# Hash-masked attention and a squared-ReLU MLP in one kernel: low planes and hash projections on the two column halves of TensorE

## The chip, the core and the metric

The kernel runs on one core of a Trainium2 chip as one launch. The metric is the device time of that launch in microseconds (us). TensorE (called PE in the profile) multiplies matrices, VectorE is DVE, ScalarE is ACT, GpSimd is POOL, and SyncE (SP) issues most of the DMAs. A matmul on PE has two instructions: a weight load, which the profile counts as an engine row of its own (PEld), and the matmul proper.

## The reference, cut to what matters

```python
q, k, v: (4, 8, 768, 64)      proj: (64, 6)
q_bits = (q @ proj > 0); k_bits = (k @ proj > 0)          # 6 bits a row
mask   = bucket(q_bits)[:, None] == bucket(k_bits)[None]   # same 6 bits
scores = where(mask, 0.125 * q @ k.T, -1e9)
attn   = softmax(scores)       # denominator + 1e-9
x      = (attn @ v)            # heads side by side: (3072, 512)
r      = maximum(x @ w_in, 0)            # w_in (512, 2048)
out    = (s * r * r + b) @ w_out         # w_out (2048, 512), float32
```

There are 32 heads (4 batches of 8), 768 rows a head, head width 64. All inputs and the output are float32, and the signs in the bits make the projections sensitive to small errors.

## The kernel before, in words

**Precision by pieces.** Most matmuls take fp16 or a rounded float32 (`F32R`). Where more precision is wanted, the kernel splits an operand into a high and a low part and multiplies the pieces one after the other: `x @ w` becomes high by high, high by low, low by high. Plain float32 (`F32`) operands go to PE as they are.

**Slots.** A head has three chunks of 256 query rows; a slot is one chunk of one head, so there are 96 slots, with two row tiles of 128 in each. A slot has a part `weights` (lines 554 to 605: scores into PSUM banks, row maximum on DVE at L574, exponential on ACT at L575, normalisation at L595 or L598) and a part `values` (lines 610 to 677: attention weights times v). Heads 0 to 9 (slots 0 to 29) are early, heads 10 to 31 late (`late(w)` is `w >= FULL`, and `FULL` is 10).

**Early values.** The attention weights are transposed on PE (L625), copied out of PSUM (L199) and multiplied in plain float32 (L632). `product(f)` does this for two key tiles at a time: key tile `m` = 0 writes output partitions 0 to 63, `m` = 1 writes 64 to 127, each with 64 weight columns, and two later instructions (L657, L658) add the halves.

**Late values.** ACT scales the normalised weights by `TOP` into an fp16 plane (L602, the high plane), DVE takes the rest as a second fp16 plane (L603, the low plane). The two planes of a row tile are one buffer of `pb`, and there are two such buffers. A DMA transpose per row tile (L604, issued by SP) brings both planes into `tb`. Then `products` (L639) issues 12 matmuls: for each of the 6 key tiles, the high plane and the low plane, each with 128 weight columns (v's high part in columns 0 to 63, v's low part in 64 to 127) and 256 moving columns.

**Preparing a head.** `prep` (lines 426 to 475) works on q and k of a head side by side, in two halves of 384 rows. `split` transposes a half on PE (L439), ACT writes the rounded part `aq` (L441), DVE the rest `bq` (L442); DMAs copy parts of these to other partitions. `hash_` then projects a half: three `F32R` matmuls of 64 weight columns and 384 moving columns (L456 to L458), and one DVE instruction (L460) turns the signs into plus or minus a huge constant in `mk`, which lies over the buffer of q and k (`nat`). After the second half, three DMAs go out (`aq` to its second place, the masks to `ks` and to `bq`), and the next head's q and k are loaded into `nat`, of which there is one. The first two heads are prepared by `prep_still`, which has matmuls of other shapes (L510 to L513). The masks ride in the second score matmul (L570) as 12 more contraction rows.

**The MLP.** `moe` (lines 684 to 750) works on 256 rows at a time. L711 to L713 are the first product in fp16 pieces, L721 to L725 the squared ReLU with its split, L736 to L738 the second product in `F32R` pieces. The MLP of a batch can start when the last head of that batch is through, and the weights are decoded and split once (lines 323 to 390).

**Order.** All steps go into a `Plan` with an engine, an assumed cost, what they read and write, and a priority; `order()` runs a list scheduler over them with these costs and issues the instructions of each engine in the order of the planned starts. The kernel is written out in that order, so on its engine an instruction that waits holds those planned behind it. The MLP has priorities above 1e5 for its matmuls, so that the planner puts them where PE would otherwise be free. `pe(cost, ...)` gives the assumed cost of a group of matmuls. In slot `i` the pieces of `prep` are called from `values` with priority `pr + PP`, where `pr` is the slot's own plus 5; the first two pieces belong to the last chunk of a head, the others to the first chunk of the next. `ering(j)` gives the buffer for the exponentials of row tile `j`: five (`NE`) in late slots, and in early slots also the two `pb` buffers, which lie idle then.

Of the kernel before, what the change touches and what calls it, by code (L numbers as in the profile page):

```python
# [139 lines left out]
def lsh_attention_moe(ctx: ExitStack, tc, q, k, v, proj, w_in, w_out, s, b, out):  # L140
# [61 lines left out]
    def mmc(n, c):  # L202
        return c * (n / 2286.0 + 0.0075)
# [17 lines left out]
    VB = [tile_(f"vb{x}", [P, NT, 2, D], F16) for x in range(2)]  # L221
    VF = [z.rearrange("p t z d -> p (t z d)")[:, 0:2 * NT * D].bitcast(F32).rearrange("p (t d) -> p t d", t=NT) for z in VB]

    NXP, NXC, NE = 3, 3, 5
    eb = tile_("eb", [P, NE, S])
    pb = tile_("pb", [P, 2, 2, S], F16)
    tb = tile_("tb", [P, 2, TPC, 2, NT, P], F16)
    PF = [[tb[:, r].rearrange("p a h t q -> p (a h t q)")[:, f * 1024:(f + 1) * 1024].bitcast(F32).rearrange("p (m q) -> p m q", m=2) for f in range(HT)] for r in range(2)]

    def late(w):  # L230
        return w >= FULL

    def TK(r, part, n):

        k = 6 // n
        return [("t", r, z) for z in range(part * k, (part + 1) * k)]
# [2 lines left out]
        return [("vb", x, z) for z in range(2)]  # L239

    pbf = pb.rearrange("p y h n -> p (y h n)").bitcast(F32)
    EB = [eb[:, x] for x in range(NE)] + [pbf[:, x * S:(x + 1) * S] for x in range(2)]
    EK = [("e", x) for x in range(NE)] + [("p", x) for x in range(2)]

    def ering(j):

        return j % NE if late(slots[j // TPC][3]) else j % (NE + 2)
    xpb = tile_("xpb", [P, NXP, CH])
    xsb = tile_("xsb", [P, 2, CH], F16)
    rb = tile_("rb", [P, 2 * CH])  # L250
# [21 lines left out]
    for z in range(2):  # L272
        for i in range(2):
            rows = slice((i ^ z) * 64, (i ^ z) * 64 + 64)
            for r in range(2):
                c = at[i] + r * NBITS
                nc.vector.tensor_scalar(pj[rows, z, c:c + NBITS], pn[rows], (1.0 if i == r else -1.0) / (1.0 if i else SCALE), None, ALU.mult)
    pj2 = tile_("pj2", [P, 2, D], F32R)
    pjh, pjl = pj2[:, 0], pj2[:, 1]
    pjs = wk.tile([P, 3, D], F32R, tag=f"w{ND_ - 1}", name="pjs")  # L280
    pjk, pjq, pjm = [pjs[:, z] for z in range(3)]
    nc.vector.tensor_copy(pjh, pj[:, 0])
    nc.vector.tensor_tensor(pjl, pj[:, 0], f32(pjh), ALU.subtract)
    nc.vector.tensor_copy(pjk[0:D], pj[0:D, 1])
    nc.vector.tensor_copy(pjk[D:P], pj[D:P, 0])
    nc.vector.tensor_tensor(pjm[0:D], pj[0:D, 1], f32(pjk[0:D]), ALU.subtract)
# [6 lines left out]
    nc.vector.memset(EB[2][0:1, 0:2 * P], 0.0)  # L293
    for i in range(2):
        for r in range(2):
            rows = slice(at[i] + r * NBITS, at[i] + (r + 1) * NBITS)
            if i != r:
                nc.vector.memset(crow[:, rows, 0], -TINY)
            nc.vector.memset(crow[:, rows, 1], BIG if i == 0 else -BIG)
    nc.scalar.dma_start(misc[:, 0:2], crow)  # L300
    nc.vector.memset(qk_sb[0:D], SCALE)
    nc.vector.memset(qk_sb[D:P], 1.0)
# [101 lines left out]
    def AK(x, r=(0, 1), g=(0, 1)):  # L404
        return [("aq", x, i, j) for i in r for j in g]

    def BK(x, r=(0, 1), g=(0, 1)):
        return [("bq", x, i, j) for i in r for j in g]
# [17 lines left out]
    def prep(w, i, pr):  # L426
        if w < STILL:
            return prep_still(w, i, pr)
        x, n = w % 2, w % NNAT
        aq, bq, ks, nat = AQ[x], BQ[x], KS[x], NAT[n]  # L430
        mk, NK, MKS = nat.rearrange("p t j d -> p (t j d)"), [("nat", n, 0), ("nat", n, 1)], [("mk", n, 0), ("mk", n, 1)]

        def split(g, i, pr):
            pb = fill_bank(i)
            cols, o = slice(g * HS, (g + 1) * HS), bank[:, pb, 0:HS]

            def tr():
                for t in range(HT):
                    nc.tensor.transpose(out=bank[:, pb, t * P:(t + 1) * P], in_=nat[:, g * HT + t], identity=ident)  # L439
            pe(0.33, tr, NK + [("mk", n, g)], [("b", pb)], pr)  # L440
            act(HS, lambda: nc.scalar.activation(aq[:, cols], o, AF.Copy, scale=qk_sb), [("b", pb)], AK(x, g=(g,)), pr, 0.12)  # L441
            dve(HS, lambda: nc.vector.scalar_tensor_tensor(bq[:, cols], o, qk_sb, f32(aq[:, cols]), ALU.mult, ALU.subtract), [("b", pb)] + AK(x, g=(g,)), BK(x, g=(g,)), pr, 0.61)  # L442
            if g:
                for z in range(2):
                    dma(lambda z=z: ks[z][0:D], lambda: aq[D:P], AK(x, r=(1,)), [("ks", x, 0, z)], pr, D * S * 4)
                dma(lambda: ks[0][D:P], lambda: bq[D:P], BK(x, r=(1,)), [("ks", x, 1, 0), ("ks", x, 1, 1)], pr, D * S * 4)

        def hash_(g, i, pr):
            pb = fill_bank(i)
            cols, o = slice(g * HS, (g + 1) * HS), bank[:, pb, 0:HS]  # L450

            n_ = KB + MR
            m, MK = mk[0:n_, cols], [("mk", n, g)]
            if not (STACK and late(w)):
                def mm():
                    nc.tensor.matmul(o[0:D], pjh, aq[:, cols], start=True, stop=False)  # L456
                    nc.tensor.matmul(o[0:D], pjl, aq[:, cols], start=False, stop=False)
                    nc.tensor.matmul(o[0:D], pjh, bq[:, cols], start=False, stop=True)  # L458
                pe(mmc(HS, 3), mm, AK(x, g=(g,)) + BK(x, g=(g,)), [("b", pb)], pr)
                dve(HS, lambda: nc.vector.tensor_scalar(m, o[0:n_], thr[0:n_], big[0:n_], ALU.is_gt, ALU.mult), [("b", pb)], MK, pr, 0.67)  # L460
            else:
                def mm():
                    for z, t in enumerate((aq, bq)):
                        nc.tensor.matmul(o, pj2.rearrange("p z c -> p (z c)"), t[:, cols], start=(z == 0), stop=(z == 1))
                pe(mmc(HS, 2), mm, AK(x, g=(g,)) + BK(x, g=(g,)), [("b", pb)], pr)
                act(HS, lambda: nc.scalar.copy(m, o[D:D + n_]), [("b", pb)], MK, pr)
                dve(HS, lambda: nc.vector.tensor_tensor(m, o[0:n_], m, ALU.add), [("b", pb)], MK, pr, 0.6)
                pool(HS, lambda: nc.gpsimd.tensor_scalar(m, m, thr[0:n_], big[0:n_], ALU.is_gt, ALU.mult), [], MK, pr, 0.7)
            if g:
                dma(lambda: aq[D:P], lambda: aq[0:D], AK(x, r=(0,)), AK(x, r=(1,)), pr, D * S * 4)  # L470
                dma(lambda: ks[1][D:HR], lambda: mk[KB:KB + MR], MKS, [("ks", x, 2, 0), ("ks", x, 2, 1)], pr, MR * S * 4)
                dma(lambda: bq[D:HR], lambda: mk[0:MR], MKS, BK(x, r=(1,)), pr, MR * S * 4)
                if w + NNAT < len(visits):
                    load(w + NNAT, pr)
        return [lambda i, pr, f=f, g=g: f(g, i, pr) for f in (split, hash_) for g in range(2)]

    def prep_still(w, i, pr):

# [75 lines left out]
    def weights(i, pr):  # L554
# [33 lines left out]
        for a in range(TPC):  # L588
            j = TPC * i + a
            e, ek = EB[ering(j)], EK[ering(j)]  # L590
            n, r = j % 2, i % 2
            hi, lo, hk = pb[:, n, 0], pb[:, n, 1], EK[NE + n]

            def norm(eng, a=a, e=e):
                eng.tensor_scalar(e, e, rz[:, a:a + 1], u[:, a:a + 1], ALU.mult, ALU.add)  # L595
            ways = [(POOL, NORM, lambda norm=norm: norm(nc.gpsimd))]
            if not late(w):
                ways.append((ACT, 0.87, lambda a=a, e=e: nc.scalar.activation(e, e, AF.Identity, bias=u[:, a:a + 1], scale=rz[:, a:a + 1])))  # L598
            plan.any(ways, [("st", y, 2), ("st", y, 3)], [ek], pr)
            if not late(w):  # L600
                continue
            act(S, lambda e=e, hi=hi: nc.scalar.mul(hi, e, TOP), [ek], [hk], pr)  # L602
            dve(S, lambda e=e, hi=hi, lo=lo: nc.vector.scalar_tensor_tensor(lo, e, TOP, hi, ALU.mult, ALU.subtract), [ek, hk], [("lo", n)], pr, 1.0)  # L603
            plan.add(SP, TCOST, lambda a=a, n=n, r=r: nc.sync.dma_start_transpose(tb[:, r, a].rearrange("p h t q -> p (h t) q"), pb[:, n].rearrange("p h n -> p (h n)")),  # L604
                     [hk, ("lo", n)], TK(r, a, 2), pr, TLAG)
# [4 lines left out]
    def values(i, pr, pieces):  # L610
# [24 lines left out]
        def products():  # L635
            t = tb[:, r]
            for kt in range(NT):
                for h in range(2):
                    nc.tensor.matmul(av, VB[x][:, kt].rearrange("p z d -> p (z d)"), t[:, :, h, kt], start=(h == kt == 0), stop=(h == 1 and kt == NT - 1))  # L639
        def between(f):  # L640
            for p_ in pieces[(f * len(pieces) + HT - 1) // HT:((f + 1) * len(pieces) + HT - 1) // HT]:
                p_(i, pr + PP)
# [3 lines left out]
                product(f)  # L646
            between(f)
        if late(w):
            pe(0.05 + 0.109 * 2 * NT, products, TK(r, 0, 1) + VK(x), [("b", 4)], pr)
        key, hh = (bb, h // 2, c), h % 2  # L650
        if hh == 0:
            xp[key] = xpb[:, nx[0] % NXP], ("xp", nx[0] % NXP)
# [144 lines left out]


FIRST = 0.8
RATE = 6.0  # L800
PACE = 2
DSTART = 3
# [5 lines left out]
TWO = 2  # L808
TCOST = 1.7
NORM = 1.1  # L810
STACK = False
TLAG = 1.5
STILL = 2
QDUP = "pool"
# [3 lines left out]
FPC = 0.62  # L818
WP = -8
MP = 0.0  # L820
PP = 0


# [24 lines left out]
```

## Time and profile before

| | |
|---|---|
| median of 3 runs | 1007.83 us (1003.64 to 1007.87) |
| profiled execution, its own time | 1006.61 us |
| its span, first to last instruction | 1004.8 us |
| mean granted PE clock | 0.969 |
| busy: PE, DVE, ACT, POOL | 944.1, 662.2, 664.4, 597.4 us |
| late products L639 | 792 matmuls, 98.9 us |
| projections L456 to L458 | 180 matmuls, 64.5 us |
| mask L460 on DVE | 60 instructions, 38.8 us |
| DMA transposes L604 | 132 |

The recorded durations of consecutive matmuls overlap (792 matmuls of L639 at a mean of 275 ns make 98.9 us busy, not 218), so the cost of a matmul in a stream is read as the distance from its start to the next start. The difference between the span and the execution's own time is 1.8 us.

### The profile page before, as it was taken

Reading aid. Unit: us, or ns where it says so; the run is one execution under the profiler, and the core shown is the slowest. Engines: PE = TensorE matmul, PEld = TensorE weight load, DVE = VectorE, ACT = ScalarE, POOL = GpSimd, SP = SyncE. Lnnn points to the kernel's source line nnn. Section 1 sums busy time; section 2 is a strip of 40 time slices with the busy share of each in tenths; the row PEclk is TensorE's granted clock in tenths of the full one; section 3 lists DMA queues with packets and bytes.
Section 4 is the critical chain, followed back from the end, with each engine's and each line's share of the span. In section 5 each row is a group of like instructions: output and inputs, shape, how many; then the busy total and the mean of one; then the engine's idle time right before and its main releaser. Section 6 shows DMA issues by size and latency. Waiting matters only on the chain.

```text
span 1004.8 us, 17499 instructions
## 1 busy us (share of the span) xinstructions
PE 944.1 (94%) x6152; PEld 750.7 (75%) x6152; DVE 662.2 (66%) x1202; ACT 664.4 (66%) x1182; POOL 597.4 (59%) x674
## 2 busy tenths in 40 slices
PE   7987796899999999979999999999999999999998
PEld 5765564566668878868888888888878888888886
DVE  6888888989877777786786788788788861000000
ACT  3787787788656677667767776777666764444442
POOL 2235645576847667767775677767675764434333
PEclk7999899799999999999999999999999999999999
DMA  4366456656328798898798989999788773101000
GB/s 102 107 176 181 137 155 158 184 153 185 97 72 152 160 192 169 163 204 160 167 190 174 169 178 187 194 175 196 158 175 188 146 152 65 42 2 42 11 23 21
DMA packets 300263, 139.68 MB, mean 139 GB/s; under 512 B 263872, under 2 KB 284864, under 8 KB 300176
## 3 DMA queue, kind: packets, MB, share of 16 engines
q1 hardware_dynamic: 294976, 121.53, 57.5%
q10 hardware_dynamic: 5200, 17.05, 5.5%
q8 instruction: 48, 0.79, 0.3%
q14 instruction: 39, 0.32, 0.1%
HBM read 48.24 MB, written 12.58 MB: 61 GB/s over the span
## 4 chain that ended last, share of the span: by engine, by line
PE 58%; issue 12%; POOL 11%; DVE 10%; DMA 5%; ACT 2%; SPq 0%; POOLq 0%; DVEq 0%; ACTq 0%
PE bank L639 8%; PE bank L569 6%; PE bank L570 5%; PE bank L711 5%; PE bank L738 5%; PE bank L736 5%; PE bank L737 5%; PE bank L712 5%; PE bank L713 5%; POOL glb L725 4%; DMA tb<-pb 3%; PE bank L625 3%; PE bank L632 3%; DVE st L574 2%; POOL rb L724 2%
## 5 line engine op out<-in xcount | busy, mean ns | idle before, releaser
L595 POOL TENSOR_SCALAR eb<-eb,st 128x768 f32<-128x768 f32 x149 | 183.1, 1234 | 71.4 <-DVE st L586 59.0
L574 DVE TENSOR_REDUCE st<-bank 128x1 f32<-128x768 f32 x192 | 181.2, 953 | 50.0 <-PE bank L570 40.2
L712 PE MATMUL bank<-xc,wi 128*128 128x256 f16 x768 | 210.4, 274 | 2.2 <-DVE wi L387 2.2
L711 PE MATMUL bank<-xc,wi 128*128 128x256 f16 x768 | 212.4, 277 | 0.0
L713 PE MATMUL bank<-xc,wi 128*128 128x256 f16 x768 | 210.4, 274 | 0.0
L575 ACT ACTIVATE eb<-bank,st 128x768 f32<-128x768 f32 x176 | 157.6, 896 | 57.0 <-DVE st L574 45.4
L603 DVE SCALAR_TENSOR_TENSOR pb<-eb,pb 128x768 f16<-128x768 f32 x132 | 147.7, 1121 | 44.2 <-ACT pb L602 42.9
L724 POOL TENSOR_SCALAR rb<-rb,misc 128x512 f32<-128x512 f32 x96 | 81.9, 853 | 144.3 <-ACT ghb L723 142.7
L569 PE MATMUL bank<-ks,aq 128*128 128x384 f32 x384 | 150.4, 392 | 10.4 <-ACT eb L575 8.8
L736 PE MATMUL bank<-w,ghb 128*128 128x512 f32 x384 | 159.9, 416 | 0.0
L738 PE MATMUL bank<-w,glb 128*128 128x512 f32 x384 | 152.3, 397 | 1.3 <-POOL glb L725 1.3
L737 PE MATMUL bank<-w,ghb 128*128 128x512 f32 x384 | 151.6, 395 | 0.0
L570 PE MATMUL bank<-ks,bq 76*128 76x384 f32 x384 | 136.1, 354 | 0.8 <-DMA bq<-nat 0.8
L602 ACT ACTIVATE pb<-eb 128x768 f16<-128x768 f32 x132 | 110.2, 837 | 35.6 <-DMA tb<-pb 21.6
L721 ACT ACTIVATE rb<-bank,dsc 128x512 f32<-128x512 f32 x70 | 48.2, 688 | 129.2 <-PE bank L713 121.6
L725 POOL TENSOR_TENSOR glb<-rb,ghb 128x512 fp32r<-128x512 f32 x96 | 130.3, 1357 | 5.7
L711 PEld LDWEIGHTS <-wi 128*128 128x128 f16 x768 | 75.4, 98 | 42.0 <-issue 35.0
L749 DVE COPY osb<-bank 128x256 f32<-128x256 f32 x4 | 1.5, 419 | 157.4 <-PE bank L738 156.8
L639 PE MATMUL bank<-tb,vb 128*128 128x256 f16 x792 | 98.9, 275 | 2.9 <-DMA tb<-pb 2.8
L579 POOL TENSOR_SCALAR st<-st 128x2 f32<-128x2 f32 x96 | 40.7, 424 | 97.7 <-DVE st L574 91.3
L569 PEld LDWEIGHTS bank<-ks,aq 128*128 128x128 f32 x384 | 76.9, 200 | 26.5 <-ACT eb L575 11.0
L639 PEld LDWEIGHTS <-vb 128*128 128x128 f16 x792 | 74.9, 98 | 22.0 <-issue 9.3
(135 smaller groups left out, 1749.4 us busy)
## 6 DMA issues: line engine op xcount, KB each, us to landing
ks<-aq SPq DMA_DIRECT2D x60, 192.0 KB
raw<-in_moe_w_in_dram ACTq DMA_DIRECT2D x16, 512.0 KB
raw<-in_moe_w_out_dram ACTq DMA_DIRECT2D x16, 512.0 KB
nat<-in_q_dram SPq DMA_DIRECT2D x32, 192.0 KB
nat<-in_k_dram SPq DMA_DIRECT2D x32, 192.0 KB
vm<-in_v_dram SPq DMA_DIRECT2D x32, 192.0 KB
xd<-xsb SPq DMA_DIRECT2D x48, 128.0 KB
xc<-xd SPq DMA_DIRECT2D x48, 128.0 KB
```

Source lines behind the costliest of these rows:

```text
L569: nc.tensor.matmul(o, aq[:, ts], ks[0][:, cols], start=True, stop=False)
L570: nc.tensor.matmul(o, bq[0:HR, ts], ks[1][0:HR, cols], start=False, stop=True)
L574: dve(S, lambda a=a, sc=sc: nc.vector.tensor_reduce(nm[:, a:a + 1], sc, AX.XY, ALU.max, negate=True), bk, [nk[a]], pr, 0.95)
L595: eng.tensor_scalar(e, e, rz[:, a:a + 1], u[:, a:a + 1], ALU.mult, ALU.add)
L639: nc.tensor.matmul(av, VB[x][:, kt].rearrange("p z d -> p (z d)"), t[:, :, h, kt], start=(h == kt == 0), stop=(h == 1 and kt == NT - 1))
L711: nc.tensor.matmul(hp, w[:, 0, fs], xc[:, 0, :], start=(cc == 0), stop=False)
L712: nc.tensor.matmul(hp, w[:, 1, fs], xc[:, 0, :], start=False, stop=False)
L713: nc.tensor.matmul(hp, w[:, 0, fs], xc[:, 1, :], start=False, stop=(cc == NC_ - 1))
L725: pool(2 * CH, lambda r=r, gh=gh, gl=gl: nc.gpsimd.tensor_tensor(gl, r, f32(gh), ALU.subtract), [rk, hk], [lk], MP)
L736: nc.tensor.matmul(o, gh[:, ts], w[:, 0], start=(f == 0), stop=False)
L737: nc.tensor.matmul(o, gh[:, ts], w[:, 1], start=False, stop=False)
L738: nc.tensor.matmul(o, gl[:, ts], w[:, 0], start=False, stop=(f == NF - 1))
```

## The change

1. **Late products.** The six high-plane matmuls stay (128 weight columns). The six low-plane matmuls now use v's high part alone: 64 weight columns, key tiles in turn on output partitions 0 to 63 and 64 to 127. The product of the low plane with v's low part is left out. The assumed cost goes from 1.358 to 1.052 us.
2. **Projections.** The two halves of a head are projected together: one group of four matmuls in plain `F32` (the unsplit `pjf`, with `aq` and `bq` read as float32), half `g` on output partitions `64 g` on. There were six `F32R` matmuls in two groups. The assumed cost is 0.72 us for a head (it was twice 0.53).
3. **Mask.** One DVE instruction on 108 partitions does both halves; there were two of 44 partitions. The threshold constants are laid out for both halves.
4. **DMAs of a head.** The mask copies go out per half: four of 18 KB in place of two of 36 KB. The copy of `aq` and the next load are as before.
5. **Buffers.** `pb` has four buffers in place of two (`NPB`); early slots get nine buffers for exponentials in place of seven. `PP` goes from 0 to -5, so the pieces of `prep` rank ahead of `values` of the same slot.

```diff
-    NXP, NXC, NE = 3, 3, 5
+    NXP, NXC, NE = 3, 3, NE_          # NE_ = 5
-    pb = tile_("pb", [P, 2, 2, S], F16)
+    pb = tile_("pb", [P, NPB, 2, S], F16)   # NPB = 4
...
-        return j % NE if late(slots[j // TPC][3]) else j % (NE + 2)
+        return j % NE if late(slots[j // TPC][3]) else j % (NE + NPB)
...
-        def hash_(g, i, pr):
+        def hash_(i, pr):
             pb = fill_bank(i)
-                def mm():
-                    nc.tensor.matmul(o[0:D], pjh, aq[:, cols], start=True, stop=False)
-                    nc.tensor.matmul(o[0:D], pjl, aq[:, cols], start=False, stop=False)
-                    nc.tensor.matmul(o[0:D], pjh, bq[:, cols], start=False, stop=True)
-                pe(mmc(HS, 3), mm, AK(x, g=(g,)) + BK(x, g=(g,)), [("b", pb)], pr)
-                dve(HS, lambda: nc.vector.tensor_scalar(m, o[0:n_], thr[0:n_], big[0:n_], ALU.is_gt, ALU.mult), [("b", pb)], MK, pr, 0.67)
...
+            def mm():
+                for z, t in enumerate((aq, bq)):
+                    for g in range(2):
+                        nc.tensor.matmul(o[g * D:(g + 1) * D], pjf, f32(t[:, g * HS:(g + 1) * HS]), start=(z == 0), stop=(z == 1))
+            pe(0.72, mm, AK(x) + BK(x), [("b", pb)], pr)
+            n_ = D + KB + MR
+            dve(HS, lambda: nc.vector.tensor_scalar(m[0:n_], o[0:n_], thr[0:n_], big[0:n_], ALU.is_gt, ALU.mult), [("b", pb)], MK, pr, 0.67)
+            dma(lambda: aq[D:P], lambda: aq[0:D], AK(x, r=(0,)), AK(x, r=(1,)), pr, D * S * 4)
+            for g in range(2):
+                cols, at_ = slice(g * HS, (g + 1) * HS), g * D
+                dma(lambda cols=cols, at_=at_: ks[1][D:HR, cols], lambda at_=at_: m[at_ + KB:at_ + KB + MR], MK, [("ks", x, 2, g)], pr, MR * HS * 4)
+                dma(lambda cols=cols, at_=at_: bq[D:HR, cols], lambda at_=at_: m[at_:at_ + MR], MK, BK(x, r=(1,), g=(g,)), pr, MR * HS * 4)
...
-            n, r = j % 2, i % 2
+            n, r = j % NPB, i % 2
...
             for kt in range(NT):
-                for h in range(2):
-                    nc.tensor.matmul(av, VB[x][:, kt].rearrange("p z d -> p (z d)"), t[:, :, h, kt], start=(h == kt == 0), stop=(h == 1 and kt == NT - 1))
+                nc.tensor.matmul(av, VB[x][:, kt].rearrange("p z d -> p (z d)"), t[:, :, 0, kt], start=(kt == 0), stop=False)
+            for kt in range(NT):
+                m = kt % 2
+                nc.tensor.matmul(av[m * D:(m + 1) * D], VB[x][:, kt, 0], t[:, :, 1, kt], start=False, stop=(kt >= NT - 2))
...
-            pe(0.05 + 0.109 * 2 * NT, products, TK(r, 0, 1) + VK(x), [("b", 4)], pr)
+            pe(0.05 + 0.109 * NT + 0.116 * HT, products, TK(r, 0, 1) + VK(x), [("b", 4)], pr)
...
-PP = 0
+PP = -5
```

More of the change, by code (lines that the diff above doesn't have):

```diff
@@ L241, in lsh_attention_moe @@
     pbf = pb.rearrange("p y h n -> p (y h n)").bitcast(F32)
-    EB = [eb[:, x] for x in range(NE)] + [pbf[:, x * S:(x + 1) * S] for x in range(2)]
-    EK = [("e", x) for x in range(NE)] + [("p", x) for x in range(2)]
+    EB = [eb[:, x] for x in range(NE)] + [pbf[:, x * S:(x + 1) * S] for x in range(NPB)]
+    EK = [("e", x) for x in range(NE)] + [("p", x) for x in range(NPB)]
     def ering(j):
-        return j % NE if late(slots[j // TPC][3]) else j % (NE + 2)
+        return j % NE if late(slots[j // TPC][3]) else j % (NE + NPB)
     xpb = tile_("xpb", [P, NXP, CH])
@@ L277, in lsh_attention_moe @@
                 nc.vector.tensor_scalar(pj[rows, z, c:c + NBITS], pn[rows], (1.0 if i == r else -1.0) / (1.0 if i else SCALE), None, ALU.mult)
-    pj2 = tile_("pj2", [P, 2, D], F32R)
-    pjh, pjl = pj2[:, 0], pj2[:, 1]
+    pjh, pjf = tile_("pjh", [P, D], F32R), tile_("pjf", [P, D])
     pjs = wk.tile([P, 3, D], F32R, tag=f"w{ND_ - 1}", name="pjs")
@@ L282, in lsh_attention_moe @@
     nc.vector.tensor_copy(pjh, pj[:, 0])
-    nc.vector.tensor_tensor(pjl, pj[:, 0], f32(pjh), ALU.subtract)
+    nc.vector.tensor_copy(pjf, pj[:, 0])
     nc.vector.tensor_copy(pjk[0:D], pj[0:D, 1])
@@ L295, in lsh_attention_moe @@
         for r in range(2):
[L296 to L299, printed above, removed]
+            for g in range(2):
+                both = slice(g * D + at[i] + r * NBITS, g * D + at[i] + (r + 1) * NBITS)
+                if i != r:
+                    nc.vector.memset(crow[:, both, 0], -TINY)
+                nc.vector.memset(crow[:, both, 1], BIG if i == 0 else -BIG)
     nc.scalar.dma_start(misc[:, 0:2], crow)
@@ L446, in split @@
                 dma(lambda: ks[0][D:P], lambda: bq[D:P], BK(x, r=(1,)), [("ks", x, 1, 0), ("ks", x, 1, 1)], pr, D * S * 4)
-        def hash_(g, i, pr):
+        def hash_(i, pr):
             pb = fill_bank(i)
[L450 to L454, printed above, removed]
-                def mm():
-                    nc.tensor.matmul(o[0:D], pjh, aq[:, cols], start=True, stop=False)
-                    nc.tensor.matmul(o[0:D], pjl, aq[:, cols], start=False, stop=False)
-                    nc.tensor.matmul(o[0:D], pjh, bq[:, cols], start=False, stop=True)
-                pe(mmc(HS, 3), mm, AK(x, g=(g,)) + BK(x, g=(g,)), [("b", pb)], pr)
[L460 to L474, printed above, removed]
@@ L475, in prep @@
-        return [lambda i, pr, f=f, g=g: f(g, i, pr) for f in (split, hash_) for g in range(2)]
+            o, m, MK = bank[:, pb, 0:HS], mk[:, 0:HS], [("mk", n, 0), ("mk", n, 1)]
+            def mm():
[4 more added lines that the diff above has]
+            n_ = D + KB + MR
@@ new lines, in hash_ @@
+            dve(HS, lambda: nc.vector.tensor_scalar(m[0:n_], o[0:n_], thr[0:n_], big[0:n_], ALU.is_gt, ALU.mult), [("b", pb)], MK, pr, 0.67)
+            dma(lambda: aq[D:P], lambda: aq[0:D], AK(x, r=(0,)), AK(x, r=(1,)), pr, D * S * 4)
+            for g in range(2):
+                cols, at_ = slice(g * HS, (g + 1) * HS), g * D
+                dma(lambda cols=cols, at_=at_: ks[1][D:HR, cols], lambda at_=at_: m[at_ + KB:at_ + KB + MR], MK, [("ks", x, 2, g)], pr, MR * HS * 4)
+                dma(lambda cols=cols, at_=at_: bq[D:HR, cols], lambda at_=at_: m[at_:at_ + MR], MK, BK(x, r=(1,), g=(g,)), pr, MR * HS * 4)
@@ L477, in prep_still @@
+            if w + NNAT < len(visits):
+                load(w + NNAT, pr)
+        return [lambda i, pr, g=g: split(g, i, pr) for g in range(2)] + [hash_]
     def prep_still(w, i, pr):
@@ L799 @@
 FIRST = 0.8
+NE_ = 5
+NPB = 4
 RATE = 6.0
@@ L810 @@
 NORM = 1.1
-STACK = False
 TLAG = 1.5
```

## The prediction

> **What bounds the kernel now.** I read the page first, then the busy time in four stretches, then who waited for whom in the late one.
>
> ```profile
> span 1004.8 us, 17499 instructions
> ...
> PE   7987796899999999979999999999999999999998
> ...
> DVE  6888888989877777786786788788788861000000
> ...
> DMA  4366456656328798898798989999788773101000
> ```
>
> ```profile
> 50.00:300.00 250.00, 209.57 (x1271) 147.82 (x1271) 213.68 (x432) 195.81 (x366) 146.91 (x161) 0.92 0.54 150
> 300.00:840.00 540.00, 532.53 (x3611) 440.50 (x3612) 409.62 (x670) 375.99 (x670) 379.03 (x426) 0.99 0.87 173
> 840.00:1005.00 165.00, 159.97 (x1053) 130.66 (x1050) 1.94 (x5) 65.81 (x95) 59.66 (x60) 1.00 0.07 22
> ```
>
> The columns are stretch, length, busy time of PE, PEld, DVE, ACT and POOL, granted clock, DMA share and GB/s. Three stages have different limits. Up to about 300 us (early heads) no engine is full: PE is busy for 209.6 of 250 us, DVE for 213.7, ACT for 195.8, and they wait on each other. From 300 to 840 (late heads, with MLP work between) PE is busy for 532.5 of 540. After 840 only the MLP is left. So from 300 on PE has no slack: what a late slot or head saves or adds there makes the end come earlier or later by as much, since the MLP behind is one backlog that PE works off. DVE at 409.6 of 540 has slack. What idle time PE has left there:
>
> ```profile
> PE bank L569 <- ACT eb L575: 2.9, 1, 2.9
> PE bank L639 <- DMA tb<-pb: 2.8, 5, 1.1
> ```
>
> **Late products (66 slots).**
>
> ```profile
> 615.82 1.47 PE L639 MATMUL bank<-tb,vb 128*128 128x256 f16 x12
> 617.04 0.42 PE L456 MATMUL bank<-aq,pj 128*64 128x384 f32 x1
> 617.30 0.33 PE L457 MATMUL bank<-aq,pj 128*64 128x384 f32 x1
> 617.47 0.34 PE L458 MATMUL bank<-bq,pj 128*64 128x384 f32 x1
> 617.65 0.33 PE L456 MATMUL bank<-aq,pj 128*64 128x384 f32 x1
> 617.82 0.33 PE L457 MATMUL bank<-aq,pj 128*64 128x384 f32 x1
> 617.99 0.33 PE L458 MATMUL bank<-bq,pj 128*64 128x384 f32 x1
> 618.17 0.28 PE L711 MATMUL bank<-xc,wi 128*128 128x256 f16 x1
> ```
>
> Twelve matmuls take 1.47 us from the first start to the last modelled end, the last lasting 0.27 (the 0.28 of the L711 row is the same shape), so a step is (1.47 - 0.27) / 11 = 0.109 us, and twelve steps are 1.31 us. After the change six stay (0.65). The six of 64 columns make three pairs; if the members of a pair run side by side, that is three steps, 0.33. Pure streaming falls to 0.98, 0.33 less a slot.
>
> The nearest row for such a pair is the early product L632: the same two output halves in turn, 256 moving columns, but plain float32.
>
> ```profile
> 225.37 1.08 PE L632 MATMUL bank<-tb,vb 128*64 128x256 f32 x8
> 226.38 0.51 PE L736 MATMUL bank<-w,ghb 128*128 128x512 f32 x1
> 226.72 0.39 PE L737 MATMUL bank<-w,ghb 128*128 128x512 f32 x1
> 226.96 0.39 PE L738 MATMUL bank<-w,glb 128*128 128x512 f32 x1
> ...
> 228.66 0.27 PE L712 MATMUL bank<-xc,wi 128*128 128x256 f16 x1
> 228.77 0.27 PE L713 MATMUL bank<-xc,wi 128*128 128x256 f16 x1
> 228.97 0.65 PE L632 MATMUL bank<-tb,vb 128*64 128x256 f32 x4
> 229.56 0.44 PE L569 MATMUL bank<-ks,aq 128*128 128x384 f32 x1
> ```
>
> The trace has two matmul instructions for each plain float32 product, so x4 is one pair and x8 two. First start to the start of what follows is 0.59 for one pair and 1.01 for two: 0.42 a pair, and 0.17 fixed. Going in costs too: L713 to L632 is 0.20, where its own step (L712 to L713) is 0.11: 0.09 more. And the first full-width matmul behind is delayed: L736 to L737 is 0.34, L737 to L738 0.24: 0.10 more (its weights come late); behind an fp16 one it would be less, so I take 0.07. A visit to the paired form thus costs 0.09 + 0.17 + 0.07 = 0.33 us above its streaming, which is just the 0.33 that the products save: 0.98 + 0.33 = 1.31.
>
> Is that 0.33 due to plain float32 or to the halves? The early rounded matmuls that go back and forth between 64 and 128 contraction rows show a cost of the same kind without plain float32:
>
> ```profile
> 16.40 0.38 PE L510 MATMUL bank<-ks,pjs 64*64 64x384 f32 x1
> 16.72 0.39 PE L511 MATMUL bank<-ks,pjs 128*64 128x384 f32 x1
> 17.03 0.38 PE L512 MATMUL bank<-bq,pj 64*64 64x384 f32 x1
> 17.34 0.39 PE L513 MATMUL bank<-aq,pjs 128*64 128x384 f32 x1
> ```
>
> Each step there is 0.31, against 0.17 for the same 384 columns in L457 to L458: 0.14 for a change of shape. The projections before (64 columns, one half only) show none: L456 to L458 go in and out of full width without a gap. I take the row nearest in form, L632: the products gain 0. Ends: -0.33 x 66 = -22 us (no cost of the visit) and +0.33 x 66 = +22 us (the visit costs 0.33 and fp16 halves don't run side by side).
>
> The Trainium skill (TensorEngine Tiling (Array Packing), Key Properties) says that a change of tiling mode, not of the tile alone, drains TensorE. The trace agrees at L632 and at L510 to L513 and shows nothing of it at L456; by that rule the products gain nothing.
>
> **Projections (30 heads, all but the first two).** Before: the products end at 615.82 + 1.31 = 617.13, L711 starts at 618.17: 1.04 us for six matmuls. After: four plain float32 matmuls of 384 columns in two pairs. L632's 0.42 is for 256, so a pair is 0.42 x 384/256 = 0.64, two are 1.28, and the visit adds 0.33: 1.61, or 0.57 more a head, 17.1 us in all. The kernel's assumed 0.72 would need half of that rate. Ends: +0.24 a head (no visit cost) and +0.57. `prep` runs two heads ahead, so heads 2 to 11 are prepared in the early slots, and 20 heads after about 300 us, where PE is full: 20 x 0.57 = +11.4. The first 10 fall where PE is busy 84%: I let half show, 10 x 0.57 / 2 = +2.9 (ends 0 and 5.7).
>
> **Mask.**
>
> ```profile
> L460 DVE TENSOR_SCALAR nat<-bank,misc 44x384 f32<-44x384 f32 x60 | 38.8, 665 | 4.0 <-PE bank L458 1.8 <-DMA ks<-bq 1.2
> L602 ACT ACTIVATE pb<-eb 128x768 f16<-128x768 f32 x132 | 110.2, 837 | 35.6 <-DMA tb<-pb 21.6 <-POOL eb L595 13.4 <-issue 0.2
> ```
>
> Thirty instructions of 0.665 go (the free size stays 384): -20 us of DVE. Late they are covered by PE, worth 0; if PE stopped being the limit there, DVE's 409.6 of 540 would come next with room. Early, DVE is busy 85%, and I let half of 10 x 0.665 show: -3.3 (ends 0 and -6.7). The new mask waits for both halves, so the first half's mask comes later; but nothing reads it before the DMAs that need both.
>
> **DMAs of a head.**
>
> ```profile
> L175 SPq DMA_DIRECT2D ks<-nat x30: 794/803/1167, 47.2 to 791.7; - x30
> L175 SPq DMA_DIRECT2D bq<-nat x30: 754/768/902, 48.2 to 793.5; - x30
> L604 SPq DMA_TRANSPOSE tb<-pb x132: 1273/1514/3169, 303.4 to 834.8; - x132
> ```
>
> These are issue times on SP in ns (least, median, most). Two more issues of about 0.78 a head are 47 us more on SP in all, about 31 of them late, where the 132 transposes alone take 132 x 1.5 = 200 us. The last mask copy leaves SP some 1.6 us later, then the load of `nat`; behind them on SP wait the transposes L604, for these L639, and in PE's order all that follows it. The wait of L639 for them is 2.8 us now. I take 0: a head's masks are needed a head later. Ends 0 and +3.
>
> **Buffers and order.** Four plane buffers take away ACT's wait for a transposed plane (21.6 us in the L602 row). ACT has slack, so only what reaches PE counts: of PE's 7.5 idle us late (540 - 532.5) I take -2, with ends 0 and -7.5. What is late next is DVE's L603 behind ACT. The early part gets two more buffers and earlier `prep`, and an earlier `prep` also sits in PE's order ahead of values when its load is late: I take 0 (ends -5 and +5).
>
> **Sum**, on the profiled execution's 1006.6 us (its span of 1004.8 and 1.8 around it; the runs' median is 1.2 higher): 0 + 11.4 + 2.9 - 3.3 + 0 - 2 + 0 = +9.0, so 1015.6, forecast 1016. Moving the small ends gives about 1004 to 1028 for this case.
>
> **Rivals.**
> A, faster: the visit cost belongs to plain float32, and fp16 halves pay none. For it: L456 to L458, at 64 columns, pay none. Against: L510 to L513 pay without plain float32, and only L632 uses both halves. Then the products save 22: 1015.6 - 22 = 994. It decides against me once a slot's products cost under 1.31 - 9/66 = 1.17 us, where the whole comes back to the time before. Chance 0.17. The Trainium skill (TensorE: Matmul & The Clock Gate, Measured speedup vs the span model) prices a pack at one matmul's duration and about 4 ns a further tile, with no cost of going in; L632's fixed 0.17 and 0.09 are not in it, and by it the time would be A's.
> B, no change: the stalls give more than I took. PE idles 40.4 us in 50:300 (250 - 209.6); if one mask, more buffers and earlier `prep` take a quarter of it, 1015.6 - 10 = 1006. Against: no single wait of PE dominates there. 0.17.
> C, slower still: fp16 halves run one after the other: +22, 1038. Against: L632's float32 pairs. Were those serial, the +17 of the projections would still hold, since it scales the measured 0.42. 0.06.
> D, the projection isn't run as the float32 form of L632, but at half of its streaming (what 0.72 needs): 0.64 + 0.33 = 0.97 a head, -0.07, so 1015.6 - 14.3 - 1.4 = 1000. Nothing in the trace shows such a rate. 0.05.
>
> **How the numbers follow.** My case has 0.50, and 0.05 is left for what I don't see. Half a per cent, 5 us, is about what a measurement of this kernel can tell from no change. Faster (under 1002.8): A and parts of B and D, 0.23. Within: most of B and the lower end of my case, 0.28. Slower: 0.49. The range 993 to 1028 holds my case, B, D and most of A, and leaves C out; my case alone is 1004 to 1028.
>
> **What would show it.** From the first product matmul of a slot to the first of what follows: 1.3 us if I am right, 1.0 under A, 1.6 under C. From the first projection matmul to what follows: 1.5 to 1.6 a head; 0.7 would break the second step. The projections should be 240 matmul instructions on PE (180 now), the products 792 as now, the mask 30. PE should stay full from 300 on; idle time growing there behind DMAs would put the end on SP. The early stage's PE idle tells B: 30 us rather than 40.

## The result, and the profile after

The changed kernel takes 1012.9 us, median of 5 runs (1010.55 to 1014.94); the kernel before took 1007.83 beside it (1003.64 to 1008.32). The ratio is 1.0061, 95% interval 1.0038 to 1.0084: slower by about 0.6%, where 1016 was forecast. The profiled execution took 1012.81 us, 6.2 more than that of before, 9.0 by the sum. It will turn out below that the PE steps of the forecast were right where they stand alone, that the projections' step is smaller where it follows the products' and is worth less at the end than on PE, and that the order of the queues, which the sum had put at nearly nothing, is worth more than all of them.

From the page after: the span, and PE, DVE and DMA in 40 slices.

```profile
span 1010.8 us, 17652 instructions
...
PE   6988886899899999979999999999999999999997
...
DVE  6779878899976677776777766776767765000000
...
DMA  4366556645448798797898799898797785101000
```

The stretches of before, now of the kernel after (busy PE, PEld, DVE, ACT, POOL, clock, DMA share, GB/s):

```profile
50.00:300.00 250.00, 214.00 (x1314) 144.15 (x1313) 215.10 (x434) 190.03 (x359) 143.95 (x159) 0.94 0.55 153
300.00:840.00 540.00, 528.08 (x3591) 405.35 (x3589) 382.99 (x632) 369.45 (x652) 369.25 (x422) 1.00 0.85 169
840.00:1011.00 171.00, 165.74 (x1099) 134.53 (x1097) 10.70 (x17) 71.15 (x105) 68.46 (x69) 1.00 0.13 34
```

The early stage is busier on PE (214.0 for 209.6), the late one has a little more idle time (11.9 for 7.5 us), and DVE now has 10.7 us of work after 840, where it had 1.9: the last late product starts at 858.1 us in place of 841.9, and the MLP behind it takes 153 us in place of 163.

A late slot's products in the timeline of PE after (start, us, line, form):

```profile
603.58 0.40 PE L733 MATMUL bank<-w,glb 128*128 128x512 f32 x1
603.82 0.83 PE L630 MATMUL bank<-tb,vb 128*128 128x256 f16 x6
604.58 0.52 PE L633 MATMUL bank<-tb,vb 128*64 128x256 f16 x6
605.03 0.50 PE L731 MATMUL bank<-w,ghb 128*128 128x512 f32 x1
605.37 0.39 PE L732 MATMUL bank<-w,ghb 128*128 128x512 f32 x1
605.60 0.40 PE L733 MATMUL bank<-w,glb 128*128 128x512 f32 x1
```

L630 are the six high planes, L633 the three pairs. From 603.82 to the next start is 1.21 us, and L731 to L732 takes 0.34 where the next step takes 0.23: 1.32 with that delay, against 1.31 before. Inside it, 604.58 - 603.82 = 0.76 is six steps of 0.109 and 0.10 on the way in; L633 to L731 is 0.45 for three steps of 0.109, and 0.12 more.

A head's projections in the same view:

```profile
599.13 0.40 PE L733 MATMUL bank<-w,glb 128*128 128x512 f32 x1
599.46 0.87 PE L456 MATMUL bank<-aq,pjf 128*64 128x384 f32 x4
600.16 0.81 PE L456 MATMUL bank<-bq,pjf 128*64 128x384 f32 x4
600.90 0.44 PE L561 MATMUL bank<-ks,aq 128*128 128x384 f32 x1
601.18 0.34 PE L562 MATMUL bank<-ks,bq 76*128 76x384 f32 x1
601.36 0.34 PE L561 MATMUL bank<-ks,aq 128*128 128x384 f32 x1
```

L733 to L456 is 0.33 (0.23 is its own step), the block takes 1.44, and L561 to L562 is 0.28 for 0.18: 0.10 + 1.44 + 0.10 = 1.64, forecast 1.61, before 1.04. But in nine of the 20 late heads the projections stand right behind a slot's pairs in PE's queue:

```profile
675.39 0.52 PE L633 MATMUL bank<-tb,vb 128*64 128x256 f16 x6
675.75 0.81 PE L456 MATMUL bank<-aq,pjf 128*64 128x384 f32 x4
676.39 0.81 PE L456 MATMUL bank<-bq,pjf 128*64 128x384 f32 x4
677.13 0.44 PE L561 MATMUL bank<-ks,aq 128*128 128x384 f32 x1
```

The three pairs take 0.36 up to the first projection, where the slot above needs 0.45 up to a full-width matmul: no way out of the narrow form, and none into it. The block takes 1.38, and 0.64 of it lies between the starts of its two pairs. One visit serves both.

The mask, the mask copies on SP and ACT's high plane, from the groups and the tile views:

```profile
L459 DVE TENSOR_SCALAR nat<-bank,misc 108x384 f32<-108x384 f32 x30 | 20.3, 676 | 24.7 <-PE bank L456 21.2 <-DMA ks<-aq 1.4 <-issue 1.2
```

```profile
L175 SPq DMA_DIRECT2D ks<-nat x60: 717/789/964, 44.7 to 811.5; - x60
L175 SPq DMA_DIRECT2D bq<-nat x60: 714/760/845, 46.5 to 820.0; - x60
```

```profile
L594 ACT ACTIVATE pb<-eb 128x768 f16<-128x768 f32 x132 | 109.2, 837 | 35.2 <-POOL eb L587 34.2
```

Thirty masks at 0.676 save 18.5 us of DVE. But DVE now stands waiting for the projections, 21.2 us in all, where the two smaller masks waited 1.8 for L458. Sixty more issues at the same price, as forecast. ACT's wait for a transposed plane (21.6) is gone and a wait for POOL's normalisation of 34.2 stands in its place: four buffers moved the wait, they didn't end it.

What PE waited for from 290 us on, after:

```profile
PE bank L733 <- POOL glb L720: 4.1, 4, 1.5
PE bank L706 <- DVE rb L716: 2.7, 2, 1.6
PE bank L561 <- ACT eb L567: 1.7, 3, 1.0
...
PE bank L630 <- DVE pb L595: 1.2, 1, 1.2
```

No transpose is in it any more (2.8 before); the MLP's own inputs are.

Where the time came up shows in the last start of the early products (360 matmuls), first and last start in the row: before, then after.

```profile
L632 PE MATMUL bank<-tb,vb x360: 379/379/689, 31.0 to 295.0; 128*64 128x256 f32 x180
```

```profile
L624 PE MATMUL bank<-tb,vb x360: 379/379/689, 30.8 to 290.1; 128*64 128x256 f32 x180
```

The early part ends 4.9 us sooner, and what follows is 1010.8 - 290.1 = 720.7 long in place of 709.8, 10.9 more. The granted PE clock differs between the two executions (0.969 before and 0.976 after, mostly early: 0.92 and 0.94 in the rows from 50 to 300 us). Over the 67 further runs of the kernel before that stand beside the runs below, the time falls by about 0.6 us for each 0.001 of mean granted clock (fitted; 0.966 to 0.981, 1001.4 to 1012.1 us). As an estimate from that, some 4 us of the difference between the two profiles are hidden by the clock.

### The profile page after: what moved, and what is told of

It reads as the page before. It is cut to its first block, busy times and chain, and to the rows that moved or that the text cites. A ratio compares the mean times of both kernels' runs of the same rounds, so it can differ in the third digit from the quotient of the medians.

```text
span 1010.8 us, 17652 instructions
## 1 busy us (share of the span) xinstructions
PE 949.7 (94%) x6212; PEld 715.1 (71%) x6212; DVE 645.1 (64%) x1181; ACT 658.3 (65%) x1170; POOL 593.4 (59%) x678
## 4 chain that ended last, share of the span: by engine, by line
PE 58%; POOL 12%; issue 12%; DVE 8%; DMA 5%; ACT 4%; SPq 1%; POOLq 0%; DVEq 0%; ACTq 0%
PE bank L561 6%; PE bank L706 5%; PE bank L733 5%; PE bank L731 5%; PE bank L562 5%; PE bank L707 5%; PE bank L708 5%; PE bank L732 5%; POOL glb L720 4%; PE bank L630 4%; PE bank L456 4%; POOL rb L719 3%; PE bank L633 3%; POOL eb L587 3%; PE bank L617 2%
## 5 line engine op out<-in xcount | busy, mean ns | idle before, releaser
L587 POOL TENSOR_SCALAR eb<-eb,st 128x768 f32<-128x768 f32 x148 | 160.5, 1089 | 62.4 <-DVE st L578 57.3
L567 ACT ACTIVATE eb<-bank,st 128x768 f32<-128x768 f32 x167 | 149.2, 894 | 54.1 <-DVE st L566 48.5
L719 POOL TENSOR_SCALAR rb<-rb,misc 128x512 f32<-128x512 f32 x96 | 86.4, 900 | 158.1 <-ACT ghb L718 155.6
L595 DVE SCALAR_TENSOR_TENSOR pb<-eb,pb 128x768 f16<-128x768 f32 x132 | 147.5, 1131 | 34.2 <-ACT pb L594 33.2
L561 PE MATMUL bank<-ks,aq 128*128 128x384 f32 x384 | 148.5, 387 | 12.5 <-ACT eb L567 9.1
L731 PE MATMUL bank<-w,ghb 128*128 128x512 f32 x384 | 160.0, 417 | 0.0
L733 PE MATMUL bank<-w,glb 128*128 128x512 f32 x384 | 152.4, 397 | 5.2 <-POOL glb L720 5.2
L732 PE MATMUL bank<-w,ghb 128*128 128x512 f32 x384 | 151.1, 393 | 0.0
L716 ACT ACTIVATE rb<-bank,dsc 128x512 f32<-128x512 f32 x78 | 53.5, 686 | 134.1 <-PE bank L708 120.5
L720 POOL TENSOR_TENSOR glb<-rb,ghb 128x512 fp32r<-128x512 f32 x96 | 134.2, 1397 | 4.8
L562 PE MATMUL bank<-ks,bq 76*128 76x384 f32 x384 | 132.5, 345 | 0.0
L594 ACT ACTIVATE pb<-eb 128x768 f16<-128x768 f32 x132 | 109.2, 837 | 35.2 <-POOL eb L587 34.2
L561 PEld LDWEIGHTS bank<-ks,aq 128*128 128x128 f32 x384 | 74.8, 195 | 45.7 <-issue 21.0
L706 PEld LDWEIGHTS <-wi 128*128 128x128 f16 x768 | 75.4, 98 | 42.1 <-issue 34.3
L733 PEld LDWEIGHTS bank<-w,glb 128*128 128x128 f32 x384 | 72.1, 188 | 24.6 <-POOL glb L720 7.9
L571 POOL TENSOR_SCALAR st<-st 128x2 f32<-128x2 f32 x96 | 35.9, 374 | 86.3 <-DVE st L566 82.0
L707 PEld LDWEIGHTS <-wi 128*128 128x128 f16 x768 | 75.9, 99 | 13.3 <-issue 4.7
```

What stands on the lines that cost most here:

```text
L561: nc.tensor.matmul(o, aq[:, ts], ks[0][:, cols], start=True, stop=False)
L562: nc.tensor.matmul(o, bq[0:HR, ts], ks[1][0:HR, cols], start=False, stop=True)
L567: act(S, lambda a=a, sc=sc, e=e: nc.scalar.activation(e.rearrange("p (g n) -> p g n", g=2), sc, AF.Exp, bias=nm[:, a:a + 1], accum_out=z[: ...
L706: nc.tensor.matmul(hp, w[:, 0, fs], xc[:, 0, :], start=(cc == 0), stop=False)
L707: nc.tensor.matmul(hp, w[:, 1, fs], xc[:, 0, :], start=False, stop=False)
L720: pool(2 * CH, lambda r=r, gh=gh, gl=gl: nc.gpsimd.tensor_tensor(gl, r, f32(gh), ALU.subtract), [rk, hk], [lk], MP)
```

## The experiments

Every kernel was timed beside the kernel before, and ratios are to that. By its ratio the changed kernel stands at +6 us. Differences between two kernels that didn't run on one chip are differences of ratios, times 1007 us.

**1. The products alone**, on the kernel before.

```diff
-  for kt: for h in range(2): matmul(av, [v high | v low], t[:, :, h, kt])
+  for kt: matmul(av, [v high | v low], t[:, :, 0, kt])
+  for kt: matmul(av[(kt % 2) * D:(kt % 2 + 1) * D], v high, t[:, :, 1, kt])
```

> The kernel before with the late products of the change alone (low planes in pairs, their assumed cost with them); projections, mask, DMAs, buffers and order as before. Theory V (a visit to the paired form costs about what the pairs save): in the trace after, a slot's products take 5 x 0.109 + 0.202 + 0.134 + 0.109 + 0.204 = 1.19 us up to the next start and delay the first full-width matmul behind by about 0.1, against 1.31 before: -0.02 to -0.04 a slot, so -1 to -3 us in all, 1005 to 1008 by the median before of 1007.8. Rival A (fp16 halves pay no visit): -22 us, 986. Rival O (the planner's lower assumed cost alone reorders the queue for the worse): +3 us or more, with PE idle time after 300 us over the 7.5 us of before.

Ratio 0.9997 (0.9976 to 1.0019). The pairs give nothing, as forecast; rival A, at 0.978, is excluded. The kernel's assumed 0.31 a slot is what streaming would save.

**2. Three visits in place of one**, on the changed kernel: the same twelve matmuls, two high planes and one low pair, three times.

> The changed kernel with the same twelve product matmuls a slot in another order: two high-plane matmuls, then one low pair, three times; so three visits to the paired form in place of one, the streaming unchanged. Theory V: each further visit costs 0.09 in, 0.02 to 0.03 for the first half weights, 0.095 out and at most 0.03 behind an fp16 matmul, 0.21 to 0.25; two more in 66 slots are +28 to +33 us, 1041 to 1046 by the changed kernel's 1012.9. Rival A2 (the gap is a fixed cost of a products group, not of going in and out): 0, 1013.

Ratio 1.0318 (1.0284 to 1.0353), +26 us by the changed kernel, 0.20 for each of the 132 further visits; expected were 28 to 33. From its timeline on PE:

```profile
606.98 0.39 PE L630 MATMUL bank<-tb,vb 128*128 128x256 f16 x2
607.30 0.30 PE L633 MATMUL bank<-tb,vb 128*64 128x256 f16 x2
607.53 0.39 PE L630 MATMUL bank<-tb,vb 128*128 128x256 f16 x2
607.85 0.30 PE L633 MATMUL bank<-tb,vb 128*64 128x256 f16 x2
...
608.64 0.44 PE L561 MATMUL bank<-ks,aq 128*128 128x384 f32 x1
```

Two full matmuls and a pair stream for 3 x 0.109 = 0.33, and the distance from one L630 group to the next is 0.55: 0.22 for going in and out. So the cost is one of the visit, and it comes as often as the form changes.

**3. All low planes at the first half**, on the changed kernel (the accumulation order is changed so that a full-width matmul ends it).

```diff
-  matmul(av[m * D:(m + 1) * D], v high, t[:, :, 1, kt])     # m = kt % 2, after six high planes
+  matmul(av[0:D], v high, t[:, :, 1, kt])                   # before the sixth high plane
```

> The changed kernel with all six low-plane matmuls on output partitions 0 to 63 (64 weight columns, no pairs), placed before the sixth high-plane matmul. Streaming is twelve steps of 0.109, 1.31 us, as in the kernel before. Theory H (the cost of a visit hangs on using the second half; 64 columns at the first half go in and out freely, as the rounded projections L456 before did): no gap, 1.31 a slot against 1.19 and 0.1 behind now, +0 to +3 us by the changed kernel, 1012 to 1016. Theory W (it hangs on the narrow weights of fp16 themselves): gaps of 0.09 on both sides and the streaming too, about +0.3 a slot, +20 us, 1033.

Ratio 1.0241 (1.0207 to 1.0274), +18 us by the changed kernel: theory W, and H is out. Its timeline:

```profile
605.32 0.72 PE L630 MATMUL bank<-tb,vb 128*128 128x256 f16 x5
605.97 0.84 PE L634 MATMUL bank<-tb,vb 128*64 128x256 f16 x6
606.75 0.28 PE L630 MATMUL bank<-tb,vb 128*128 128x256 f16 x1
```

Five full steps are 0.545 and the way to L634 takes 0.65: 0.10 in. Six matmuls on one half take 0.78 up to the next start, 0.65 of streaming and 0.13 more. They don't run side by side, and they pay for going in and out though the second half is never used. So in fp16 it is 64 weight columns that cost. The rounded float32 projections of before also have 64 columns and pay nothing (617.04 to 618.17 in the prediction); the halves in plain float32 pay. Why the rounded form is exempt no run here shows. The Trainium skill (TensorEngine Tiling (Array Packing), Key Properties) has a drain at a change of tiling mode; the fp16 and plain float32 rows agree with it, the rounded rows L456 to L458 do not.

**4. The projections, mask and mask copies alone**, on the kernel before (two plane buffers, `PP` 0).

> The change's projections, single mask and four mask DMAs alone; products as before, two plane buffers, no shift of prep's priority. Theory V: 1.42 us from first projection matmul to the next start, 0.09 on the way in and up to 0.1 behind, against 1.04 before, so +0.5 to +0.57 a head; 20 late heads count in full, the early ones half, less half of the early mask gain: +8 to +12 us, 1016 to 1020. Rival S (early stalls decide, the projections are hidden): within 3 us of before, 1005 to 1011. Rival O (the rest is the planner's order): any value, but then PE idle after 300 us differs by more than 4 us from the kernel before.

Ratio 1.0166 (1.0134 to 1.0198), +16.7 us: above the 8 to 12 that theory V expected, far above S, and without the sign of O (PE is idle for 10.4 us from 300 to 840, 2.9 more than before). None of the three holds.

**5. The same kernel with other projections.** Six rounded matmuls of 128 weight columns, in which 64 zero columns stand beside the 64 of the projection, so that each half of a head lands on its place; no plain float32 and no 64 columns. The assumed cost stays, and so the order on all engines.

```diff
-  for z, t in enumerate((aq, bq)): for g in range(2):
-      matmul(o[g * D:(g + 1) * D], pjf, f32(t[:, half g]))
+  for g in range(2): for w, t in ((high, aq), (low, aq), (high, bq)):
+      matmul(o, [w | 0] if g == 0 else [0 | w], t[:, half g])
```

> The kernel with the change's projections alone (1022.7, +16 by the kernel before), in its own order of instructions, but the projections as six rounded matmuls of 128 padded columns, as in the two runs before. Single mask and four mask DMAs stay, products, buffers and order are as before the change. Theory V (in that kernel too the projections' time on PE is what costs, by as much as in the changed kernel's order): -7, 1014 to 1017, and the other +9 is the planner's order. Theory E (all of the +16 is the projections' time on PE, since nothing else is in that kernel to hide it): 1005 to 1009. Theory O (all is order): 1019 to 1023.

Ratio 1.0082 (1.0061 to 1.0103): 8.5 us less, nearest to theory V. So the projections' time on PE is worth 8.5 us there, and the other 8 lie in what is left of the edit: one late mask, four copies, and the order that the planner makes of them. These weren't separated.

**6 and 7. The padded projections in the changed kernel**, first with an assumed cost of 1.05, then with the changed kernel's 0.72.

> The changed kernel with the projections as six rounded matmuls of 128 weight columns, where the weights of one half of the head are padded with 64 zero columns, so that both halves' outputs come to the same places as in the change, without plain float32 and without a visit to the paired form. Single mask, four mask DMAs, products, buffers and order stay. Theory V: 6 x 0.175 = 1.05 us a head against 1.34 + 0.09 + 0.1 on both sides and up to 1.6, so -0.4 to -0.55 a head over 20 late heads and part of the early ones: -8 to -14 us by the changed kernel, 999 to 1005. Rival (the 5 us of the change come from the queue's order, not from the projections): 1010 to 1015.

Ratio 1.0111 (1.0086 to 1.0137): slower than the changed kernel by 5 us although PE has some 0.5 us a head less to do. A miss, and the reason was that the new assumed cost made a new order. With the old one:

> The run with projections of 128 padded columns once more, but with the changed kernel's assumed 0.72 for them, so that every engine has its instructions in the changed kernel's order; only what the projections take on PE differs. In the run before this one the assumed cost was 1.05, the planner found another order, and PE's idle time grew. Theory V: -0.4 to -0.55 a head over 20 late heads and half of that early, -8 to -14 us by the changed kernel's 1012.9: 999 to 1005. Rival L (where PE is late, the others are less late: a part of what the projections cost is taken from waits): -2 to -7, 1006 to 1011. Rival: over 1013, then the projections' PE time is not what costs.

Ratio 0.9990 (0.9971 to 1.0009), 7 us below the changed kernel, between what L (up to 7) and V (from 8) expected. The projections in its timeline:

```profile
592.47 0.40 PE L739 MATMUL bank<-w,glb 128*128 128x512 f32 x1
592.70 0.52 PE L462 MATMUL bank<-aq,pjw 128*128 128x384 f32 x2
593.05 0.34 PE L462 MATMUL bank<-bq,pjw 128*128 128x384 f32 x1
593.23 0.52 PE L462 MATMUL bank<-aq,pjw 128*128 128x384 f32 x2
593.58 0.34 PE L462 MATMUL bank<-bq,pjw 128*128 128x384 f32 x1
593.76 0.34 PE L567 MATMUL bank<-ks,aq 128*128 128x384 f32 x1
```

1.06 us from 592.70 to 593.76, and no gap on either side: against 1.64, 0.58 a head. Its early part ends at 286.6:

```profile
L630 PE MATMUL bank<-tb,vb x360: 379/379/689, 31.2 to 286.6; 128*64 128x256 f32 x180
```

3.5 us sooner than in the changed kernel, and from there to the end of its span of 1002.5 are 715.9 us, 4.8 less than in the changed kernel, where 20 heads x 0.58 would be 11.6. Where a head's projections stood behind the pairs, the pairs now pay for their own way out, and the head gains only 0.24. So PE is busy for 695.2 us of this part, 7.9 less than in the changed kernel (703.1), and idle for 3.1 more: 4.8 at the end. The granted clock of the early part is 0.92 in both.

**8. No 64 columns in late slots**: run 7 with the twelve full-width product matmuls of before, in the same order.

> The same, and the late products as the twelve full-width matmuls of the kernel before, with the changed kernel's assumed cost, so again in its order. No fp16 or plain float32 pair is left in late slots. Theory V: the products cost about 0.02 to 0.04 a slot more than in pairs, so within +3 us of the run without that edit. If the pairs had a hidden cost (weights of the next matmul late, or the products' last step later for ACT and DVE), it is faster by more than 3 us.

Ratio 1.0017 (0.9994 to 1.0040), +2.7 us by run 7 with overlapping intervals. The pairs are worth 2.7 us, give or take about 3, and are not a hidden loss.

**9. Buffers and order alone**, on the kernel before (`NPB` 4, `PP` -5).

> Four plane buffers (nine early exponential buffers) and the earlier priority of prep alone; projections, mask, DMAs and products as before. Theory V: what the change measures below the sum of its PE terms comes from here: -2 to -6 us, 1002 to 1006, with PE idle shrinking in the first 300 us. Rival S0 (buffers and order do nothing): within 1.5 us of before.

Ratio 1.0044 (1.0024 to 1.0065): slower, where all theories had it equal or faster. Its early products:

```profile
L632 PE MATMUL bank<-tb,vb x360: 378/379/689, 31.5 to 287.6; 128*64 128x256 f32 x180
```

7.4 us sooner than before (295.0). But it isn't the waits that shrank there, as the busy time of PE and its clock show, before and then in this run (stretch, length, busy, clock, DMA share, GB/s):

```profile
0.00:295.00 295.00, 246.90 (x1463) 0.91 0.52 143
0.00:287.60 287.60, 238.84 (x1447) 0.94 0.53 144
```

PE is idle for 48.1 us before and 48.8 here. Nearly the same matmuls took 8.1 us less at a higher granted clock, and this profile has the highest mean clock of its kernel's twelve runs (0.981; the others 0.970 to 0.975, one 0.978). So this row doesn't show that buffers and order gain anything early. The rest is 1008.0 - 287.6 = 720.4 long, 10.6 more, of which about 2 us are MLP and score matmuls that were done earlier before. What PE waits for from 290 us on:

```profile
PE bank L639 <- DMA tb<-pb: 6.9, 6, 4.1
PE bank L569 <- DVE bq L442: 2.6, 4, 1.1
PE bank L569 <- DVE nat L460: 1.9, 4, 1.0
```

The transposes (2.8 before) and `prep`'s own DVE work have become late for PE: these three rows are 7.8 us more than before, and PE's idle time there is 7.1 more (19.7 for 12.6).

**10 and 11. The changed kernel with `PP` back at 0, and with two plane buffers.**

> The changed kernel with PP back at 0 (prep ranked behind values of its slot, as before); four plane buffers, pairs and projections stay. The parts alone gave 0 (products), +16 (projections, mask, DMAs) and +4.5 (buffers and order), 20 in sum, where the whole change gives 5 to 6: some 15 us come from buffers or order only where the joint projection is there. Theory P (the earlier rank of prep gives them, since the joint projection and its single mask come later in a head): without it 1018 to 1025. Theory N (the buffers give them): 1010 to 1015, as the changed kernel.

> The changed kernel with two plane buffers (seven early exponential buffers) in place of four, PP at -5. Theory N (the extra buffers give the 15 us that the parts alone don't show): 1018 to 1025. Theory P (the rank of prep gives them): 1010 to 1015, as the changed kernel. If both this and the run with PP at 0 land near 1013, the sum of parts isn't a matter of either, but of what order the planner happens to find.

Ratios 1.0407 (1.0374 to 1.0439) and 1.0157 (1.0139 to 1.0176): 35 and 10 us above the changed kernel. So neither is without effect: N's time came out, and P's effect is more than twice the 15 us that it was made for. The shift and the buffers, which together cost the kernel before something, are what keeps the joint projection from costing much more. In the run with `PP` at 0 PE waits from 290 us on:

```profile
PE bank L561 <- ACT eb L567: 11.5, 7, 2.8
PE bank L733 <- POOL glb L720: 6.1, 7, 1.5
PE bank L630 <- DMA tb<-pb: 5.1, 6, 1.9
```

**12. The changed kernel, with the measured costs told to the planner.**

```diff
-  pe(0.72, ...)                                 # a head's projections
+  pe(1.6, ...)
-  pe(0.05 + 0.109 * NT + 0.116 * HT, ...)       # a slot's products, 1.05
+  pe(1.3, ...)
```

> The changed kernel's instructions with the costs that the trace shows told to the planner: 1.6 us for a head's projections (0.72 assumed) and 1.3 for a slot's products (1.05). Work on PE is the same, only the order changes. Theory M (the wrong costs make a bad order): faster than the changed kernel by 3 us or more, 1010 or less. Theory N (the order is a matter of small luck): anywhere from 1003 to 1035, with the difference lying in PE's idle time and not in its work. Theory 0 (the order doesn't matter): within 2 us of 1012.9.

Ratio 1.0221 (1.0196 to 1.0247), +16 us with not one instruction more: N's time, and M is out. Its early part ends at 299.3, 9.2 later:

```profile
L624 PE MATMUL bank<-tb,vb x360: 379/379/689, 33.3 to 299.3; 128*64 128x256 f32 x180
```

But N's other half fails, that the difference would lie in PE's idle time. PE's 6212 matmuls are busy for 960.3 us where the changed kernel has 949.7, which is 10.6 of the 16.1 us between the two profiles. Up to 299.3 us the granted clock is low:

```profile
0.00:299.30 299.30, 252.23 (x1473) 0.89 0.51 141
```

In the changed kernel it is 0.92 up to 290.1, with 246.6 us of busy time. All five runs of this version have a mean clock of 0.962 to 0.966, and the five of the changed kernel 0.973 to 0.978. So with the order not only the waits changed but also the clock that PE was granted; how the one leads to the other no run here shows.

None of these versions is faster than the kernel before beyond its interval; run 7 is level with it.

## Why the prediction came out right, and what in it was wrong

- **The bound.** That PE sets the time after 300 us holds only in part. What an edit adds to PE there does come out at the end, but not in full, and `PP` alone made what follows the early products 24.7 us longer (run 10: 745.4 us from 297.8 on, where the changed kernel has 720.7), in a stage where I had called PE's slack 7.5. The clock, which differs with the order too (run 12), was in no term.
- **Products: 0.** Right, measured 0 (run 1), with the visit at 0.22 and about 0.1 behind it, forecast 0.33. The choice between the two nearest rows, L632 and L456, was the right one, and runs 2 and 3 show why: fp16 behaves like L632.
- **Projections: +11.4 late and +2.9 early.** Right to 2% on PE for a head that goes into the paired form by itself (1.64 for 1.61 us). Early 3.5 us by run 7's stage, close. Late is the term that was mis-sized: 4.8 by the profile of run 7, not 11.4, and 7 to 8.5 for both stages together by the ratios (runs 5 and 7), where the sum had 14.3. It took a visit for each head, but nine of the 20 late heads share one with the products, so run 7 takes only 7.9 us of busy time off PE; 3.1 of these come back as waits. That one visit can serve two groups was not in the prediction.
- **Mask: -3.3.** Not seen. DVE's instructions got fewer as forecast, but DVE stood 21.2 us waiting for the joint projection; that "nothing reads it before" the copies was true and beside the point, since DVE's queue stood behind it. Up to 290 us, where the gain was expected, nine masks take 6.1 us (before, 18 take 11.9) and wait 5.3 us for L456 (before, 0.6 for L458). Whether any gain is left is open, since mask, copies and order were not run apart; together they cost 8 us in run 5.
- **DMAs: 0, buffers: -2, order: 0.** The prices were right (0.76 to 0.79 an issue; the wait for transposes gone), the effect was not: buffers and order give +4.4 alone (run 9), and where the joint projection is there the order (`PP`) is worth -35 (run 10) and the buffers -10 (run 11). The ends that I gave them, -7.5 and -5 to +5, were too narrow by far.
- **The sum.** +9.0 against +6.2 by the profiles, from a projection term twice too large and order terms taken as nearly nothing. The parts alone add up to 0 + 16.7 + 4.4 = 21 and the whole is 6: the terms don't add, and each of these edits also gave the planner another order. So the time came out right in part by luck: of what moved it most, the forecast had the size of neither the order nor the clock.
- **Rivals.** A is out by runs 1 and 3, C by the three steps of the pairs in 0.45 us, D by 1.44 us a block. Of B's mechanism a part is there: PE idles 36.0 us from 50 to 300, where B had 30 and my case 40. The early part ended 4.9 us sooner, but at a higher granted clock, so that this can't all be put down to fewer waits; run 9's earlier end has no fewer waits at all.

## What to carry to other kernels

Count what it costs to go into a narrow form and out of it, not only its streaming: here 0.2 to 0.3 us a visit, so three pairs of 0.109 us just pay for themselves, and a pair block is worth having only where many pairs follow each other. Narrow groups that stand next to each other in the queue share a visit. A kernel whose order comes from a planner must be compared in the same order: keep the assumed costs while the instructions change, or the order's own luck (12 us between runs 6 and 7, 16 in run 12, 35 in run 10) hides a term of 7. Compare the granted clocks too before reading a stage's length off two profiles. And see what a merged instruction makes its queue wait for, before counting the instruction that it saves.

## What the runs showed of the hardware that I had not expected

- Six fp16 matmuls of 64 weight columns on one half take about 0.11 us each ((0.84 - 0.27) / 5 in L634's row), as much as with 128, and still pay 0.10 going in and 0.13 going through and out (run 3). Rounded float32 with 64 columns pays neither.
- Padding the weights with zero columns to full width costs nothing measurable on PE: 1.06 us for six rounded matmuls of 128 columns (run 7), 1.04 for six of 64 before.
- A plain float32 pair of 384 columns costs the 0.64 us that scaling L632's 0.42 gives (675.75 to 676.39): two pairs, the first weights and the way out are 1.44 us from first start to next start.
- fp16 pairs and plain float32 pairs that follow each other need one way in and one way out together: 0.36 us from L633 to L456 for three pairs, and 0.45 from L633 to a full-width matmul.
